# One hand-written list of single steps for the last pass, the drain and the start of the experts

## Chip, cores and metric

The kernel runs on one core of one Trainium2 chip. The metric is device time of the core in microseconds (us); the time of the kernel before is the median of three runs.

## The reference, cut to what matters

```python
def reference(**kwargs):
    attn_out = _attn_ref(q, k, v)            # B, H, S, D = 8, 8, 576, 64
    x = attn_out.transpose(0, 2, 1, 3).reshape(B * S, H * D)     # 4608 tokens x 512
    return _moe_ref(x, w_gate, w1, w2)

def _attn_ref(q, k, v):                      # two attentions, added
    out_d = sm_attn(mean over 4 of q, k, v)  # 144 x 144 scores for each head
    out_up = np.repeat(out_d, 4, axis=2)
    scores = scale * q @ k.T, masked to |i - j| < 4
    return out_up + softmax(scores) @ v

def _moe_ref(x, w_gate, w1, w2):             # 8 experts, one for each token
    e = argmax(x @ w_gate); gate = softmax(x @ w_gate)[e]
    return gate * (relu(x @ w1[e]) @ w2[e])  # 512 -> 1024 -> 512
```

## The kernel before

The attention handles 32 pairs of heads, one pair i in each pass. `steps(i)` (L813) walks the table `PASS` (L805) once; each entry is a function with an offset, so that one pass works on four pairs at different stages: scores of pair i (`s_loc` L256, `s_d` L310), exponentials of pair i-1 (`exp_d` L327), transposes of pair i-2 (`t_loc` L336, `t_d` L350, evicted by `e_loc` L343 and `e_d` L357), and products with v of pair i-3 (`pv_loc` L364, `pv_d` L378), whose result `out_d` (L385, ScalarE) and `add_up` (L389, VectorE) add into the token tile XT. Entries with "@" are hooks for routing work (`route_a`, `route_b`, `route_s`, `route_c`, L407 to L475), for turning token tiles (`x_rows` L477: four transposes on TensorE into a PSUM tile `pX`, then one ScalarE copy into the buffer `xr`), for the scatter of a token tile to the experts' rows in DRAM (`scatter` L502, an indirect DMA that GpSimd issues), and for the loads of q and k (`load_after` L125).

After pass 31, three more calls of `steps` drain the pipeline (pairs 29 to 31). Between them stands, written out by hand, the routing of the last batch m = 3 (token tiles 0 to 3, `first`; 4 to 8, `rest`) and the first half of expert 0: rows 0 to 255, whose tokens came from earlier batches. `x_load` (L543) reads these rows back from DRAM, `prep` (L585) turns them (`x_turn` L570, a VectorE transpose) and splits them into a high part on ScalarE (L576) and a low part on VectorE (L577), and `s1` (L621) multiplies them with w1, twelve matmuls for each of eight slices f. `split_w2` (L611) splits the weights of the second product. Then `s2` (L668) makes the second product for token tiles 0 and 1, while `x_load(0, 1)` reads rows 256 to 639, which need every scatter; `prep(0, 2, 3, 4)` turns those, and the loop over the experts starts with `s1` on rows 256 to 511.

The order on each engine is the order in the program; the framework only adds semaphore waits. Tiles of one name take turns in a fixed number of buffers (`pX` has three PSUM banks, `pPV` one pair of banks, `p1` two), and a writer waits for the last reader of the buffer. Memory of closed pools is used again, so `x_load(0, 0)` needs pools of the attention closed. The rows of `xr` of the last batch's tiles 4 to 8 take two places that its tiles 2 and 3 have filled, so the two small writes of `route_c` into them (L472 on ScalarE, L473 on VectorE) wait for the scatters of tiles 2 and 3 to land.

Of the kernel before, what the change touches and what calls it, by code (L numbers as in the profile page):

```python
# [22 lines left out]
NP = B * H // 2  # L23
N, DM, E, F = B * S, H * D, 8, 1024
# [14 lines left out]
FIRST = 512  # L39
# [47 lines left out]
EARLY = slice(0, CH[0][1])  # L87
# [3 lines left out]
def attention_moe_kernel(ctx: ExitStack, tc: tile.TileContext, qk, vw, wg, w1, w2, cst, csb, out):  # L91
# [17 lines left out]
    def bank():  # L109
        return psX.tile([128, 512], F32, name="pX", bufs=3)  # L110
# [293 lines left out]
    def x_slot(m, t):  # L404
        return t if t < 4 else t - 4 if m < B // 2 - 1 else t - 9 + NX
# [15 lines left out]
    def route_b(m, tiles):  # L421
        T = len(tiles)
        lg = RS[m, "lg"]
        p = bank()
        nc.tensor.transpose(p[:, :128], lg[:, :128], ident)
        if T > 4:
            nc.tensor.matmul(p[:, 128:160], lg[:, 128:], cf[:, C_SUM:C_SUM + 32], start=True, stop=True)
        pl = p[:, :T * 32].rearrange("p (t e) -> p t e", e=32)[:, :, :E]
        m_ = rp.tile([128, 5], F32, name="rm")
        nc.vector.tensor_reduce(m_[:, :T], pl, axis=AX.X, op=OP.max)  # L430
        d = p[:, 256:296].rearrange("p (t e) -> p t e", e=E)
        nc.vector.tensor_sub(d[:, :T], pl, m_[:, :T, None].to_broadcast([128, T, E]))
        ex = rp.tile([128, 5, E], F32, name="re")
        nc.scalar.activation(ex[:, :T], d[:, :T], AF.Exp)  # L434
        RS[m, "ex"], RS[m, "p"] = ex, (p, m_)

    def route_s(m, tiles):
        T = len(tiles)
        p, m_ = RS[m, "p"]
        d = p[:, 256:296].rearrange("p (t e) -> p t e", e=E)  # L440
        sc = p[:, 320:360].rearrange("p (t e) -> p t e", e=E)
        nc.vector.scalar_tensor_tensor(sc[:, :T], d[:, :T], 0.0,
                                       cf[:, None, C_DESC:C_DESC + E].to_broadcast([128, T, E]),
                                       op0=OP.is_ge, op1=OP.mult)
# [29 lines left out]
        for j, t in enumerate(tiles):  # L474
            IDX[m, t] = ix[:, j:j + 1]  # L475

    def x_rows(m, t):  # L477
        p = bank()
        for k in range(4):
            nc.tensor.transpose(p[:, k * 128:(k + 1) * 128], XT[m][:, k, t * 128:(t + 1) * 128], ident)  # L480
        xr = xrs[:, x_slot(m, t)]
        nc.scalar.activation(xr[:, :DM].rearrange("p (b k d) -> p k b d", k=4, d=32),
                             p.rearrange("p (k b d) -> p k b d", k=4, d=32), AF.Copy)

    prev_sc = []

# [359 lines left out]
    for i in range(NP):  # L846
        load_vw(i)
        if i == 0:
            for h in range(3):
                load_qk(2, h)  # L850
        if i == 2:
            nc.gpsimd.tensor_copy(crun, cf[:, C_CAP:C_CAP + E])
        if i in PADS:
            pad_first(PADS.index(i))
        if i == 8:
            nc.sync.dma_start(xs[0:ROW0, :], pad)
        steps(i)
        if i + 1 < len(WARM):
            warm(WARM[i + 1], i >= 3)
        if i == NP - 1:  # L860
            close_p1.close()
            close_s.close()
            _, mp[0] = pool(name="m1", bufs=1)
            _, mp["p1"] = pool(name="psM1", bufs=2, space=PSUM)
            x_load(0, 0)
            gi_load(0, 0, 2)
            raw_ahead(8)
# [5 lines left out]
    route_s(m, first)
    x_rows(m, 2)
    x_rows(m, 3)
    prep(0, 0, 1, get=h_bank)
    steps(NP + 1)
    s1(0, 0, EARLY)
    gi_make(0, 0, 2)
    steps(NP + 2)  # L880
    steps(NP + 3)
    route_a(m, rest)
    route_c(m, first)
    for t in (2, 3, 0, 1):
        scatter(m, t)
    route_b(m, rest)
    route_s(m, rest)
    x_rows(m, 6)
    x_rows(m, 7)
    s1(0, 1, EARLY)  # L890
    route_c(m, rest)
    x_rows(m, 8)
    s1(0, 2, EARLY)
    x_rows(m, 4)
    split_w2(0, 0)
    s1(0, 3, EARLY)
    x_rows(m, 5)
    for f in (4, 5, 6, 7):
        s1(0, f, EARLY)
        if f == 4:  # L900
            for t in rest:
                scatter(m, t)
        for j in (2 * f - 7, 2 * f - 6):
            if j < 6:
                split_w2(0, j)
# [100 lines left out]
```

## Time and profile before

| | |
|---|---|
| median of 3 runs | 646.76 us (643.39, 646.76, 649.69) |
| the profiled execution | 650.97 us |
| its span, first to last instruction | 649.2 us |
| TensorE busy | 623.0 us (96%) |
| VectorE busy | 362.8 us (56%) |
| ScalarE busy | 328.5 us (51%) |
| GpSimd busy | 186.6 us (29%) |
| mean granted TensorE clock | 0.990 of full speed |

Pass 31 begins with the first matmul of `s_loc(31)` at 180.23 us of the span; the first half of expert 0 ends at 216.02 us. A share of busy time is an average over the whole span: what a change in one stretch is worth is read from the waits of that stretch. The granted clock has two levels, 1.00 (2.4 GHz) and 0.50 (1.2 GHz).

### The profile page before, as it was taken

Reading aid. Unit: us, or ns where it says so; the run is one execution under the profiler, and the core shown is the slowest. Engines: PE = TensorE matmul, PEld = TensorE weight load, DVE = VectorE, ACT = ScalarE, POOL = GpSimd, SP = SyncE. Lnnn points to the kernel's source line nnn. Section 1 sums busy time; section 2 is a strip of 40 time slices with the busy share of each in tenths; the row PEclk is TensorE's granted clock in tenths of the full one; section 3 lists DMA queues with packets and bytes.
Section 4 is the critical chain, followed back from the end, with each engine's and each line's share of the span. In section 5 each row is a group of like instructions: output and inputs, shape, how many; then the busy total and the mean of one; then the engine's idle time right before and its main releaser. Section 6 shows DMA issues by size and latency. Waiting matters only on the chain.

```text
span 649.2 us, 16208 instructions
## 1 busy us (share of the span) xinstructions
PE 623.0 (96%) x6296; PEld 515.4 (79%) x6299; DVE 362.8 (56%) x658; ACT 328.5 (51%) x885; POOL 186.6 (29%) x271
## 2 busy tenths in 40 slices
PE   7999999999989989999999999999999999999994
PEld 3777777888868888888888888888888888888873
DVE  5998889999973465571481075175138156125020
ACT  3777778988974354452462263254236154224120
POOL 6635667778823410111111101110111101110111
PEclk9999999999998989999999999999999999999998
DMA  9799888899852695274284258238238628010001
GB/s 323 244 241 293 248 285 282 274 311 303 260 145 107 147 326 148 89 189 146 75 213 147 66 156 218 67 113 206 80 92 216 181 83 222 34 47 1 34 19 41
DMA packets 74962, 108.28 MB, mean 167 GB/s; under 512 B 16442, under 2 KB 40394, under 8 KB 74846
## 3 DMA queue, kind: packets, MB, share of 16 engines
q1 hardware_dynamic: 68718, 87.63, 47.1%
q0 software_dynamic: 5984, 19.01, 7.9%
q8 instruction: 66, 1.08, 0.7%
q14 instruction: 50, 0.41, 0.2%
q10 hardware_dynamic: 144, 0.15, 0.1%
HBM read 86.98 MB, written 23.41 MB: 170 GB/s over the span
## 4 chain that ended last, share of the span: by engine, by line
PE 76%; issue 8%; DMA 6%; DVE 3%; POOL 2%; ACT 2%; SPq 1%; POOLq 0%; another core or an unknown queue 0%; DVEq 0%; ACTq 0%
PE p L630 8%; PE p L631 8%; PE p L629 8%; PE p L643 7%; PE p L645 7%; PE p L644 7%; PE pD L317 4%; PE pPV L382 2%; PE pX L341 2%; PE pX L354 2%; PE pPV L369 2%; PE pS L268 2%; DMA xs<-xr,ix 2%; PE pX L725 2%; PE pX L744 2%
## 5 line engine op out<-in xcount | busy, mean ns | idle before, releaser
L629 PE MATMUL p<-xh,w1h 128*128 128x512 f32 (+1 forms) x288 | 106.8, 371 | 1.5 <-ACT xh L576 1.5
L630 PE MATMUL p<-xl,w1h 128*128 128x512 f32 (+1 forms) x288 | 106.3, 369 | 0.8 <-DVE xl L577 0.8
L631 PE MATMUL p<-xh,w1l 128*128 128x512 f32 (+1 forms) x288 | 106.3, 369 | 0.0
L643 PE MATMUL p<-w2h,hh 128*128 128x512 f32 x256 | 101.2, 395 | 0.0
L645 PE MATMUL p<-w2h,hl 128*128 128x512 f32 x256 | 99.8, 390 | 0.0
L644 PE MATMUL p<-w2l,hh 128*128 128x512 f32 x256 | 99.7, 390 | 0.0
L650 POOL DMA_INDIRECT out_dram<-y,tix x39 | 37.9, 971 | 215.1 <-ACT y L662 203.7
L634 DVE SCALAR_TENSOR_TENSOR hl<-p,hh 128x512 fp32r<-128x512 f32 (+1 forms) x72 | 45.5, 631 | 92.0 <-ACT hh L633 91.7
L633 ACT ACTIVATE hh<-p 128x512 fp32r<-128x512 f32 (+1 forms) x72 | 39.6, 551 | 77.6 <-PE p L631 77.6
L662 ACT ACTIVATE y<-p,gi 128x512 f32<-128x512 f32 x32 | 22.0, 689 | 94.1 <-PE p L645 89.8
L629 PEld LDWEIGHTS p<-xh,w1h 128*128 128x128 f32 x288 | 55.2, 192 | 11.0 <-ACT xh L576 2.0
L630 PEld LDWEIGHTS p<-xl,w1h 128*128 128x128 f32 x288 | 55.3, 192 | 9.6 <-DVE xl L577 0.9
L631 PEld LDWEIGHTS p<-xh,w1l 128*128 128x128 f32 x288 | 55.3, 192 | 8.8
L228 POOL TENSOR_TENSOR qkt<-qk 128x864 f32<-128x864 f32 (+2 forms) x33 | 52.5, 1590 | 20.4 <-DMA qk<-in_qk_dram 17.5
L645 PEld LDWEIGHTS p<-w2h,hl 128*128 128x128 f32 x256 | 48.0, 188 | 10.3
L644 PEld LDWEIGHTS p<-w2l,hh 128*128 128x128 f32 x256 | 48.1, 188 | 10.0 <-DVE w2l L619 0.5
L643 PEld LDWEIGHTS p<-w2h,hh 128*128 128x128 f32 x256 | 48.1, 188 | 9.4
L505 POOL DMA_INDIRECT xs<-xr,ix x36 | 36.2, 1006 | 41.6 <-ACT re L434 11.1
L619 DVE TENSOR_TENSOR w2l<-raw,w2h 128x512 fp32r<-128x512 f32 x64 | 43.4, 680 | 2.2 <-DMA xs<-xr,ix 1.5
L577 DVE TENSOR_TENSOR xl<-pX,xh 128x512 fp32r<-128x512 f32 x38 | 24.6, 683 | 35.2 <-ACT xh L576 34.2
L208 ACT ACTIVATE w1h<-raw 128x512 fp32r<-128x512 f32 (+1 forms) x72 | 41.8, 581 | 0.0
L209 DVE TENSOR_TENSOR w1l<-raw,w1h 128x512 fp32r<-128x512 f32 x56 | 39.4, 704 | 0.8
(149 smaller groups left out, 1183.3 us busy)
## 6 DMA issues: line engine op xcount, KB each, us to landing
raw<-in_w_dram SPq DMA_DIRECT2D x59, 512.0 KB
vw<-in_vw_dram SPq DMA_DIRECT2D x32, 320.0 KB
qk<-in_qk_dram SPq DMA_DIRECT2D x32, 293.0 KB
qk<-in_qk_dram SPq DMA_DIRECT2D x32, 290.0 KB
qk<-in_qk_dram SPq DMA_DIRECT2D x32, 288.0 KB
xrow<-xs SPq DMA_DIRECT2D x32, 192.0 KB
xrow<-xs SPq DMA_DIRECT2D x32, 128.0 KB
xs<-xs SPq DMA_DIRECT2D x6, 512.0 KB
```

The source lines that it names most:

```text
L208: nc.scalar.activation(hi[:, s], src[:, s], AF.Copy)
L209: (nc.vector if quarters is None else nc.gpsimd).tensor_sub(lo[:, s], src[:, s], hi[:, s])
L228: nc.gpsimd.tensor_add(QKT[i][:, a:a + n], sl(0), sl(1))
L619: nc.vector.tensor_sub(lo, src, hi)
L629: nc.tensor.matmul(p, wh[:, fs], xh[:, k, r], start=(k == 0), stop=False)
L630: nc.tensor.matmul(p, wh[:, fs], xl[:, k, r], start=False, stop=False)
L631: nc.tensor.matmul(p, wl[:, fs], xh[:, k, r], start=False, stop=(k == 3))
L633: nc.scalar.activation(hh[:, f, r], p, AF.Relu)
L634: nc.vector.scalar_tensor_tensor(hl[:, f, r], p, 0.0, hh[:, f, r], op0=OP.max, op1=OP.subtract)
L643: nc.tensor.matmul(p, hh, wh, start=(f == 0), stop=False)
L644: nc.tensor.matmul(p, hh, wl, start=False, stop=False)
L645: nc.tensor.matmul(p, hl, wh, start=False, stop=(f == 7))
```

## The change

Pass 31, the three drain passes, the routing of the last batch and the first half of expert 0 become one tuple `FIN` of 117 single steps, called one after the other; `y` is pair 30 and `z` pair 31. Passes -1 to 30 still go through `PASS`. To make single steps, `x_rows` is cut into its transposes (`x_turned`) and its copy (`x_put`), `prep` of tiles 0 and 1 into its turn (`x_early`) and its split (`split_early`), and the closing of the attention's pools with the first loads of the experts becomes the step `open_moe`, where the tiles of `XH` and `HT` are now taken too, so that addresses stay. The three tiny DMAs of pass 31 that held back loads of q and k (L129; there is nothing left to hold back) fall away. Everything from `totals()` on is as before. The scatters of the last batch go out in the order 1, 3, 2, 0, 6, 7, 8, 4, 5 (before: 2, 3, 0, 1, 4, 5, 6, 7, 8).

```diff
-    def x_rows(m, t):
-        p = bank()
+    def x_turned(m, t):
+        p = BX["x", m, t] = bank()
         for k in range(4):
             nc.tensor.transpose(p[:, k * 128:(k + 1) * 128], XT[m][:, k, t * 128:(t + 1) * 128], ident)
-        xr = xrs[:, x_slot(m, t)]
-        nc.scalar.activation(xr[:, :DM].rearrange("p (b k d) -> p k b d", k=4, d=32),
-                             p.rearrange("p (k b d) -> p k b d", k=4, d=32), AF.Copy)
+
+    def x_put(m, t):
+        nc.scalar.activation(xrs[:, x_slot(m, t), :DM].rearrange("p (b k d) -> p k b d", k=4, d=32),
+                             BX.pop(("x", m, t)).rearrange("p (k b d) -> p k b d", k=4, d=32), AF.Copy)
...
-        steps(i)
+        if i < NP - 1:
+            steps(i)
...
-        if i == NP - 1:
-            close_p1.close()
...
+    def open_moe():
+        close_p1.close()
+        close_s.close()
+        _, mp[0] = pool(name="m1", bufs=1)
+        _, mp["p1"] = pool(name="psM1", bufs=2, space=PSUM)
+        x_load(0, 0)
+        gi_load(0, 0, 2)
+        x_tiles(0, 0)
+        h_tiles(0)
+        raw_ahead(8)
...
-    steps(NP)
-    route_b(m, first)
...
+    def x_early(t):
+        turned[t] = prep(0, t, get=h_bank, hold=True)
+
+    def split_early(t):
+        turned.pop(t)()
+
+    FIN = (
+        (s_loc, z), (scatter, 2, 8), (max_loc, z), (pv_d, y - 2), (t_loc, y - 1, 0), (t_loc, y - 1, 1), (sub_loc, z),
...
+    )
+    for f, *a in FIN:
+        f(*a)
     totals()
```

The two orders on VectorE, from the end of the first routing step of the last batch. `x_turn` is the STREAM_TRANSPOSE from `xrow`, the two L396 are `add_up` of pairs 30 and 31, L462 to L473 are `route_c` of tiles 0 to 3. Before:

```order
L447 TENSOR_TENSOR oh<-pX,rm 128x32
L572 STREAM_TRANSPOSE p_4441<-xrow_4345 128x4x4x32
L572 STREAM_TRANSPOSE p_4443<-xrow_4345 128x4x4x32
L577 TENSOR_TENSOR xl_4440<-p_4441,xh_4439 128x4x128
L577 TENSOR_TENSOR xl_4440<-p_4443,xh_4439 128x4x128
L396 TENSOR_TENSOR XT<-pPV,outd_122 128x580
L634 SCALAR_TENSOR_TENSOR hl<-p_4499,hh 128x256
L396 TENSOR_TENSOR XT<-pPV,outd_123 128x580
L462 TENSOR_TENSOR pX<-pX,oh 128x32
```

The same place on VectorE now (line numbers from L480 on have grown by up to 11):

```order
L447 TENSOR_TENSOR oh<-pX,rm 128x32
L577 STREAM_TRANSPOSE p_4468<-xrow_4350 128x4x4x32
L396 TENSOR_TENSOR XT<-pPV,outd_122 128x580
L582 TENSOR_TENSOR xl_4358<-p_4468,xh_4357 128x4x128
L577 STREAM_TRANSPOSE p_4492<-xrow_4350 128x4x4x32
L462 TENSOR_TENSOR pX<-pX,oh 128x32
L464 TENSOR_REDUCE gt<-re 128x4
L466 TENSOR_REDUCE pX<-pX 128x4
L469 CAST ix<-pX 128x4
L473 RECIPROCAL xr<-gt 128x4
L396 TENSOR_TENSOR XT<-pPV,outd_123 128x580
L582 TENSOR_TENSOR xl_4358<-p_4492,xh_4357 128x4x128
```

One transpose instead of two transposes and two subtractions now stands ahead of `add_up` of pair 30, and `route_c` of the first tiles has moved ahead of `add_up` of pair 31.

TensorE from the first routing transpose (L425, `route_b`) on; L480 are `x_rows` or `x_turned`, L369 and L382 `pv_loc` and `pv_d`, L341 and L354 `t_loc` and `t_d`, L629 the first `s1` of expert 0. Before:

```order
L425 MATMUL pX<-cf,lg 128x128
L480 MATMUL pX<-cf,XT 128x128 x8
L369 MATMUL pPV<-AT,vw 64x58 x20
L382 MATMUL pPV<-ADT,vds 64x144 x4
L341 MATMUL pX<-cf,A 128x128 x5
L354 MATMUL pX<-cf,AD 72x112 x6
L629 MATMUL p_4499<-xh_4439,w1h_2070 128x256
```

TensorE from the same transpose now; L455 begins `route_c` of the first tiles:

```order
L425 MATMUL pX<-cf,lg 128x128
L369 MATMUL pPV<-AT,vw 64x58 x20
L480 MATMUL pX<-cf,XT 128x128 x4
L382 MATMUL pPV<-ADT,vds 64x144 x4
L354 MATMUL pX<-cf,AD 72x112 x6
L341 MATMUL pX<-cf,A 128x128 x5
L480 MATMUL pX<-cf,XT 128x128 x4
L382 MATMUL pPV<-ADT,vds 64x144 x4
L455 MATMUL pX<-crun,onesf 128x40
```

The transposes of pair 31 are followed by `pv_d` of pair 31 and by the routing, and the first `s1` has moved behind `pv_loc` of pair 31 and `route_a` of the last tiles.

## Rows read from the trace of the kernel before

**Rows 1.** The page, busy time of TensorE: share of the span, instructions.

```profile
PE 623.0 (96%) x6296; PEld 515.4 (79%) x6299; DVE 362.8 (56%) x658; ACT 328.5 (51%) x885; POOL 186.6 (29%) x271
```

**Rows 2.** Waits of TensorE after 180 us, the four longest: total us, times, longest.

```profile
PE pX L354 <- ACT AT L348: 2.9, 2, 2.3
PE p L629 <- ACT xh L576: 1.5, 1, 1.5
PE p L630 <- DVE xl L577: 0.8, 1, 0.8
PE pX L414 <- DVE XT L396: 0.6, 1, 0.6
```

**Rows 3.** Windows: length, busy time of five engines, granted clock, DMA share, GB/s.

```profile
7.00:15.00 8.00, 5.69 (x82) 3.68 (x85) 5.28 (x9) 3.52 (x13) 5.29 (x6) 1.00 1.04 397
45.00:80.00 35.00, 32.11 (x771) 26.89 (x769) 30.92 (x63) 27.60 (x102) 19.29 (x23) 1.00 0.89 270
...
196.19:199.60 3.41, 3.41 (x55) 3.08 (x55) 0.42 (x1) 0.38 (x1) 0.00 (x0) 0.50 0.09 32
...
227.69:230.32 2.63, 0.38 (x1) 0.19 (x1) 2.63 (x6) 2.34 (x4) 0.40 (x1) 1.00 1.08 291
230.32:233.73 3.41, 3.38 (x16) 3.38 (x17) 0.78 (x2) 0.64 (x3) 1.55 (x4) 0.50 1.03 411
```

**Rows 4.** Timeline of TensorE: start, length in us, line, what, idle time before.

```profile
180.23 0.33 PE L262 MATMUL pS<-cb 64*64 64x320 bf16 x4
...
182.89 0.45 PE L354 MATMUL pX<-cf,AD 112*72 112x112 f32 x3
...
195.25 0.48 PE L354 MATMUL pX<-cf,AD 112*72 112x112 f32 x3 [2.28 <-ACT AT L348]
...
210.00 0.39 PE L629 MATMUL p<-xh,w1h 128*128 128x256 f32 x1
...
216.02 0.28 PE L518 MATMUL pX<-crun,onesf 128*128 128x8 f32 x2
...
227.30 0.39 PE L645 MATMUL p<-w2h,hl 128*128 128x512 f32 x1
229.22 0.38 PE L629 MATMUL p<-xh,w1h 128*128 128x256 f32 x1 [1.53 <-ACT xh L576]
230.35 0.58 PE L630 MATMUL p<-xl,w1h 128*128 128x256 f32 x1 [0.75 <-DVE xl L577]
```

**Rows 5.** Timeline of VectorE around the turn of expert 0's first rows.

```profile
189.86 0.81 DVE L303 TENSOR_TENSOR A<-A,pD 128x640 f32<-128x640 f32 x1
...
192.69 1.32 DVE L572 STREAM_TRANSPOSE p<-xrow 128x512 f32<-128x512 f32 x2 [0.64 <-DMA xrow<-xs]
...
195.33 0.75 DVE L396 TENSOR_TENSOR XT<-pPV,outd 128x580 f32<-128x580 f32 x1
```

**Rows 6.** The chain that ended last, from 181 us to 221 us.

```profile
181.55 1.08 ACT AD L331 x6
182.64 5.37 DMA xs<-xr,ix
188.06 0.34 SPq L541
...
194.53 0.41 ACT outd L386
...
216.11 4.30 DMA xs<-xr,ix
220.76 0.33 SPq L541
```

**Rows 7.** All that touches the scattered rows, 175 to 235 us: time to landing.

```profile
DMA to landing us min/median/max: 3.0/3.6/5.4
```

**Rows 8.** Timeline of GpSimd: two of the nine scatters of the last batch.

```profile
205.42 0.96 POOL L505 DMA_INDIRECT xs<-xr,ix  x1 [0.22 <-issue]
...
210.25 0.96 POOL L505 DMA_INDIRECT xs<-xr,ix  x1 [1.14 <-ACT xr L482]
```

More of the change, by code (lines that the diff above doesn't have):

```diff
@@ L475, in route_c, with x_rows @@
             IDX[m, t] = ix[:, j:j + 1]
-    def x_rows(m, t):
-        p = bank()
+    def x_turned(m, t):
+        p = BX["x", m, t] = bank()
         for k in range(4):
             nc.tensor.transpose(p[:, k * 128:(k + 1) * 128], XT[m][:, k, t * 128:(t + 1) * 128], ident)
-        xr = xrs[:, x_slot(m, t)]
-        nc.scalar.activation(xr[:, :DM].rearrange("p (b k d) -> p k b d", k=4, d=32),
-                             p.rearrange("p (k b d) -> p k b d", k=4, d=32), AF.Copy)
+    def x_put(m, t):
+        nc.scalar.activation(xrs[:, x_slot(m, t), :DM].rearrange("p (b k d) -> p k b d", k=4, d=32),
+                             BX.pop(("x", m, t)).rearrange("p (k b d) -> p k b d", k=4, d=32), AF.Copy)
+    def x_rows(m, t):
+        x_turned(m, t)
+        x_put(m, t)
     prev_sc = []
@@ L583, in attention_moe_kernel, with x_tiles @@
     XB = {}
+    def x_tiles(e, c):
+        if (e, c) not in XH:
+            XH[e, c] = tuple(mp[c].tile([128, 4, FIRST if c == 0 else 128], F32R, name=f"x{w}{c}") for w in "hl")
     def prep(e, *ts, get=bank, hold=False):
@@ L588, in prep @@
             c, s = chunk(t)
-            if (e, c) not in XH:
-                XH[e, c] = tuple(mp[c].tile([128, 4, FIRST if c == 0 else 128], F32R, name=f"x{w}{c}") for w in "hl")
+            x_tiles(e, c)
             r = min(t // 2, 1)
@@ L619, in split_w2, with h_tiles, s1 @@
         nc.vector.tensor_sub(lo, src, hi)
-    def s1(e, f, r=slice(0, FIRST)):
+    def h_tiles(e):
         if e not in HT:
             HT[e] = tuple(mp[0].tile([128, 8, FIRST], F32R, name=f"h{w}") for w in "hl")
+    def s1(e, f, r=slice(0, FIRST)):
+        h_tiles(e)
         xh, xl = XH[e, 0]
@@ L856, in attention_moe_kernel @@
             nc.sync.dma_start(xs[0:ROW0, :], pad)
-        steps(i)
+        if i < NP - 1:
+            steps(i)
         if i + 1 < len(WARM):
             warm(WARM[i + 1], i >= 3)
-        if i == NP - 1:
-            close_p1.close()
[L862 to L867, printed above, removed]
+    def open_moe():
[8 more added lines that the diff above has]
+        raw_ahead(8)
@@ L868, in attention_moe_kernel @@
     m = B // 2 - 1
     first, rest = list(range(4)), list(range(4, 9))
-    steps(NP)
-    route_b(m, first)
[L873 to L905, printed above, removed]
+    y, z = NP - 2, NP - 1
+    turned = {}
+    def x_early(t):
+        turned[t] = prep(0, t, get=h_bank, hold=True)
+    def split_early(t):
+        turned.pop(t)()
@@ new lines, in attention_moe_kernel @@
+    FIN = (
+        (s_loc, z), (scatter, 2, 8), (max_loc, z), (pv_d, y - 2), (t_loc, y - 1, 0), (t_loc, y - 1, 1), (sub_loc, z),
+        (exp_d, y), (x_turned, m, 0), (out_d, y - 2), (pv_loc, y - 2), (s_d, z), (t_d, y - 1, 0), (sums, y),
+        (eps, y), (add_up, y - 2), (e_loc, y - 1, 0), (e_loc, y - 1, 1), (t_d, y - 1, 1), (inv, y), (x_put, m, 0),
+        (e_d, y - 1, 0), (t_v, z), (pv_loc, y - 1), (scatter, 2, 7), (max_d, z), (open_moe,), (e_v, z),
+        (e_d, y - 1, 1), (norm, y), (norm_d, y), (max_scale, z), (exp_loc, z), (exp_d, z), (t_loc, y, 0),
+        (t_d, y, 0), (pv_d, y - 1), (t_d, y, 1), (sums, z), (out_d, y - 1), (t_loc, y, 1), (e_d, y, 0),
+        (add_up, y - 1), (e_loc, y, 0), (eps, z), (inv, z), (norm_d, z), (e_loc, y, 1), (e_d, y, 1),
+        (gi_make, 0, 0, 2), (route_b, m, first), (norm, z), (pv_loc, y), (x_turned, m, 1), (pv_d, y), (t_d, z, 0),
+        (t_d, z, 1), (x_put, m, 1), (route_s, m, first), (t_loc, z, 0), (out_d, y), (x_early, 0), (t_loc, z, 1),
+        (x_turned, m, 3), (add_up, y), (e_d, z, 0), (e_d, z, 1), (e_loc, z, 1), (pv_d, z), (split_early, 0),
+        (e_loc, z, 0), (x_early, 1), (out_d, z), (x_put, m, 3), (route_c, m, first), (pv_loc, z), (x_turned, m, 2),
+        (add_up, z), (split_early, 1), (scatter, m, 1), (route_a, m, rest), (x_turned, m, 6), (x_put, m, 2),
+        (x_put, m, 6), (s1, 0, 0, EARLY), (route_b, m, rest), (scatter, m, 3), (scatter, m, 2), (route_s, m, rest),
+        (s1, 0, 1, EARLY), (x_turned, m, 7), (x_put, m, 7), (route_c, m, rest), (split_w2, 0, 0), (split_w2, 0, 1),
+        (x_turned, m, 4), (s1, 0, 2, EARLY), (x_turned, m, 8), (scatter, m, 0), (x_put, m, 8), (s1, 0, 3, EARLY),
+        (x_put, m, 4), (scatter, m, 6), (split_w2, 0, 2), (x_turned, m, 5), (x_put, m, 5), (s1, 0, 4, EARLY),
+        (split_w2, 0, 3), (scatter, m, 7), (split_w2, 0, 4), (scatter, m, 8), (scatter, m, 4), (s1, 0, 5, EARLY),
+        (s1, 0, 6, EARLY), (scatter, m, 5), (s1, 0, 7, EARLY), (split_w2, 0, 5),
+    )
```

## The prediction

> **What bounds the kernel now.** I read the page first: TensorE is busy 96% of the span [rows 1], so only time in which TensorE stands still, or runs at half clock, can be won by a new order of the same instructions. The waits of TensorE come next, from pass 31 to the end of the span [rows 2]: the four longest kinds, 5.8 us together, all lie in the rewritten stretch or in what hangs on it. The windows view then shows what the waits cost beyond themselves [rows 3]: after the longest one (2.28 us, ending at 195.25 [rows 4]) the granted clock stands at 0.50 for 3.41 us, and after the pair of waits that ends at 230.35 again for 3.41 us. At half clock a stretch does half its work, so each costs 3.41 / 2 = 1.7 us. The budget of the change is therefore 2.9 + 0.6 us of waits in the drain, 1.7 us of clock behind them, 1.5 + 0.8 us of waits before expert 0's second half, and 1.7 us of clock behind those: 9.2 us, 1.4% of the profiled execution's 650.97 us.
>
> The first place, in order of time: the second wait for L348 [rows 2, 4] ends at 195.25. ScalarE's evictions and VectorE's `add_up` of pair 30 stood behind the turn of expert 0's first rows. Those rows came back from DRAM at 192.69, and VectorE then made two transposes and two subtractions before `add_up` could start at 195.33 [rows 5]: 2.64 us. The second place: the last scatter starts at 216.11, while `s1` ends at 216.02 (L518 begins there) [rows 4, 6]. The read of rows 256 to 639 starts on SP at 220.76, after that scatter has landed [rows 6], and its split product reaches TensorE at 230.35, 2.7 us after TensorE had finished at 227.30 + 0.39 = 227.69 [rows 4].
>
> **The change, part by part.** TensorE gets the same matmuls, so its work costs and saves nothing in itself. The three dropped DMAs of pass 31 held back nothing, since no load is left behind them except the read of expert 0's rows, which waits longer for the scatters: nothing.
>
> *Waits in the drain.* Before: 3.5 us. Now, one by one:
> - `add_up(30)` has one transpose ahead of it, not 2.64 us of work. The read of the rows starts at 188.06, after the scatter begun at 182.64 has landed [rows 6]. That scatter and the one ahead of it change places; the new first one needs the later of two copies on ScalarE, done when the exponentials begin at 181.55 [rows 6], so the pair runs up to 0.3 us later. Rows at 192.7 to 193.0, a transpose of 1.32 / 2 = 0.66, `add_up` of 0.75 [rows 5]: TensorE's `pv_d(31)` can start at 194.1 to 194.4. TensorE gets there at about 193.4: it stood still from 192.97 with almost the same matmuls behind it, and I add 0.4 for the new waits below. Wait: 0.7 to 1.0 us, I take 0.8 where there were 2.28.
> - The shorter wait for L348, 2.9 - 2.3 = 0.6 us, was for one of three `pX` banks; the new order asks for banks as fast, so 0.6 stays.
> - `route_a` waited 0.6 us for `add_up(31)`; four transposes now lie between, so 0.
> - New: `pv_d(28)` goes ahead of `pv_loc(28)`, and the latter then waits for `out_d(28)`, which reads the same bank and stands behind the exponentials on ScalarE (181.55 + 1.08 = 182.63, and its own run of 0.41 [rows 6]). TensorE was at 182.89 after four groups [rows 4], and one of these is now a little shorter: it is ready at 182.7. Wait 0.3. Behind it queue the scores of pair 31 and everything else; the next evictions have the same 0.3 of slack.
> - New: the transposes of pair 30 follow VectorE's normalisation more closely (0.81 us long [rows 5]); half of one, 0.4, is my estimate, between 0 and 0.8.
>
> New waits: 0.8 + 0.6 + 0 + 0.3 + 0.4 = 2.1, a gain of 1.4. If the rows land early and the small ones vanish, 0.9 is left (gain 2.6); if all are double, 4.2 (loss 0.7).
>
> *The clock in the drain.* The longest single wait falls from 2.28 to 0.8. From 7 to 15 us TensorE has 8.00 - 5.69 = 2.3 us of idle time and a clock of 1.00 [rows 3]. So I expect no half-clock stretch: 1.7 gained; the other end is 0.
>
> *The last scatters.* One `s1` of 256 rows takes (216.02 - 210.00) / 4 = 1.5 us [rows 4]. In both orders six of them and three groups of transposes come after the `route_c` of tiles 4 to 8, so that `route_c` ends about 10.2 us before the end T of the last `s1`, and its small writes are ready at T - 9.3. Before, they had to wait for the scatter of tile 3, begun at 205.42 [rows 8], to land, and then the first of the five scatters was that of tile 4, whose copy came last but one: it began at 210.25, T - 5.8 [rows 8]. Now tile 2's scatter follows a copy made ahead of the first `s1`, at about T - 13.8; with 3.0 to 5.4 us to landing [rows 7] the gate opens between T - 9.3 and T - 8.4, and tiles 6 and 7 go first, whose copies are long done. Five scatters took 216.11 - 210.25 = 5.9 us from first to last start [rows 6, 8]. The last now starts between T - 3.4 and T - 2.5, before T + 0.1: earlier by 2.6 to 3.5 us against the end of `s1`. The rows were 2.7 us late. So the 2.3 us of waits go, and what is late next is nothing on TensorE, with 0 to 0.8 us to spare; a remainder of a tenth or two may stay. The half-clock stretch behind them goes too, 1.7 us. The other end is 0 for both.
>
> Other scatters, copies and weight splits that moved cost nothing in the sum: they lie on engines that are 29 to 56% busy [rows 1], beside eight `s1` of 1.5 us each. If that cover failed, `s1` would wait for `hl` two slices later.
>
> The sum: 1.4 + 1.7 + 2.3 + 1.7 = 7.1 us off the profiled execution, 650.97 to 643.9. That execution is 0.65% above the median of the runs shown, so the same share gives 646.76 x 643.9 / 650.97 = 639.7 us.
>
> One rule would move the first term. The scatters here took 3.0 to 5.4 us to land [rows 7]. The Trainium skill (DMA: Bandwidth & Descriptors, Anatomy of one DMA) puts the fixed cost of such a DMA at about 2 us; by that the rows would be back before `add_up(30)` needs VectorE, the 0.8 would be gone and the time be 638.9. No scatter in that stretch landed so fast, so I keep the row.
>
> **Rivals.**
> 1. *The clock in the drain still drops.* Several waits of 0.3 to 0.8 us within 10 us may do what one of 2.28 did. Against it: 45 to 80 us has 2.9 us of idle time, clock 1.00 [rows 3]. Then 1.4 + 2.3 + 1.7 = 5.4 us: 641.4.
> 2. *The rows of the second half stay late.* If one of the last copies on ScalarE stands behind a weight split or a blocked write, or the scatters stretch, the last scatter starts near T as before. For it: scatter and splits share the end of the list, and the spare is under 1 us. Then only 1.4 + 1.7 = 3.1 us: 643.7.
> 3. *Slower: the clock stays low through the drain.* With waits spread over the whole stretch, TensorE would sit at 0.50 not for one stretch but from the first wait at 183 us on. Each 3.41 us costs 1.7; against the 5.4 us of the other terms the change loses from the fourth stretch on, and 1% from the seventh; eight cover 27 us, up to the end of the first half: 8 x 1.7 - 5.4 = 8.2 us, 655.0. Both low stretches of the trace follow waits of over 2 us together, and 45 to 80 us argues against it [rows 3]. The Trainium skill (TensorE: Matmul & The Clock Gate, A second HAM failure mode: psum-queue depth-cycling) says that short idle times between groups of matmuls, from cycling through PSUM banks, can make the clock swing; this drain cycles through three banks, but no row here shows it.
> 4. *The new order costs as much as it saves* in waits that I do not see, an undone first term and a leftover of the second: 645 to 646.
>
> **How the numbers follow.** Forecast 0.57, rival 1 0.14, rival 2 0.18, rival 3 0.05, rival 4 0.06. The three runs shown spread by 1%, and 1% (6.5 us) is about what a measurement can tell from no change. The forecast's 7.1 us is just past that line, with about 2 us of doubt: 0.67 of it falls beyond, of rival 1 a third, of rival 2 little: 0.57 x 0.67 + 0.14 x 0.33 + 0.18 x 0.1 = 0.45. Slower gets rival 3 and a bit of rival 4, 0.06; the rest, 0.49, is within 1%. The range goes from gains of 8.7 us and a fast run, 636.0, to rival 2 with a slow run, 645.5.
>
> **What would show it.** Right: no wait of TensorE over 1 us between 180 and 240 us; clock 1.00 throughout that stretch; the last scatter at least 2.5 us before the end of the last `s1`, which ends near 213; `s1` of the second half beginning straight behind `s2`, some 6 us of it earlier. Wrong: a half-clock stretch after 185 us, a wait of L640 or L641 for `xh` or `xl` near 225 us, or a TensorE wait on `out_d`, `A` or a bank of over 1 us.

## The result, and the profile after

| | before | now |
|---|---|---|
| median, first comparison (4 runs each) | 646.85 us | 641.34 us |
| ratio, with 95% interval | | 0.9886 [0.9845, 0.9928] |
| median, second comparison (35 and 12 runs) | 646.73 us | 639.1 us |
| ratio, with 95% interval | | 0.9881 [0.9855, 0.9907] |
| the profiled execution | 650.97 us | 641.42 us |
| its span | 649.2 us | 639.6 us |

The change is 1.2% faster, 7.6 us by the second comparison; the prediction was 639.7 us. One of the 12 runs, and one of the six of x10 below, was disturbed and is left out of the ratios and means. TensorE has the same matmuls and is busy for nearly the same time: 621.0 us for 623.0. The two half-clock stretches had made 2 x 1.7 us of those; this execution has one of its own at 13.1 us, in code that is the same in both kernels. The page's busy row, which answers to [rows 1]:

```profile
PE 621.0 (97%) x6299; PEld 513.5 (80%) x6299; DVE 363.2 (57%) x658; ACT 329.7 (52%) x885; POOL 185.8 (29%) x271
```

The longest kinds of waits of TensorE after 178 us (total us, times, longest), which answer to [rows 2]:

```profile
PE pX L736 <- DVE xb L775: 0.4, 1, 0.4
PE pX L341 <- ACT ADT L362: 0.4, 1, 0.4
PE p L640 <- issue: 0.3, 1, 0.3
PE pX L341 <- ACT mxd L325: 0.2, 1, 0.2
```

None of the four kinds of [rows 2] is left. The two for `pX` of L341 lie in the drain, with two smaller ones of 0.08 and 0.13 us that both wait for `out_d`; the others lie at 611 and 253 us, far behind the change. The windows (length, busy time of five engines, granted clock, DMA share, GB/s) answer to [rows 3]; the first reaches from the start of pass 31 to the start of `s2`, the others over the two places where the clock had been at 0.50:

```profile
179.03:210.67 31.64, 30.84 (x477) 27.06 (x477) 21.66 (x52) 23.06 (x69) 12.56 (x26) 1.00 0.50 170
183.00:195.00 12.00, 11.28 (x212) 8.30 (x212) 10.20 (x25) 10.28 (x34) 0.20 (x2) 1.00 0.74 226
218.00:228.00 10.00, 10.00 (x70) 9.34 (x70) 7.04 (x12) 5.55 (x12) 2.41 (x6) 1.00 1.07 355
```

The whole stretch from pass 31 to `s2` is at full clock, and TensorE idles 31.64 - 30.84 = 0.8 us of it (before: 35.93 - 32.31 = 3.6). The timeline of TensorE (start, length, line, what, idle time before) answers to [rows 4]; L654 is the first product of `s2`, L640 and L641 the first `s1` of expert 0's second half:

```profile
179.03 0.33 PE L262 MATMUL pS<-cb 64*64 64x320 bf16 x4
...
187.62 0.44 PE L341 MATMUL pX<-cf,A 128*128 128x128 f32 x2 [0.40 <-ACT ADT L362]
...
192.07 0.72 PE L382 MATMUL pPV<-ADT,vds 72*64 72x144 f32 x8
...
210.67 0.47 PE L654 MATMUL p<-w2h,hh 128*128 128x512 f32 x1
...
221.45 0.39 PE L656 MATMUL p<-w2h,hl 128*128 128x512 f32 x1
221.68 0.28 PE L640 MATMUL p<-xh,w1h 128*128 128x256 f32 x1
221.79 0.28 PE L641 MATMUL p<-xl,w1h 128*128 128x256 f32 x1
```

I call the start of pass 31 S and the start of `s2` T. From S to T it was 216.16 - 180.23 = 35.93 us and is 210.67 - 179.03 = 31.64. From T to the first product with `xl` of the second half (T to `xl` below) it was 230.35 - 216.16 = 14.19 us and is 221.79 - 210.67 = 11.12. VectorE's timeline answers to [rows 5], and for the second half's rows shows how close they come:

```profile
190.54 0.73 DVE L577 STREAM_TRANSPOSE p<-xrow 128x512 f32<-128x512 f32 x1
191.18 0.74 DVE L396 TENSOR_TENSOR XT<-pPV,outd 128x580 f32<-128x580 f32 x1
192.54 0.69 DVE L582 TENSOR_TENSOR xl<-p,xh 128x512 fp32r<-128x512 f32 x1 [0.63 <-ACT xh L581]
...
218.31 1.91 DVE L577 STREAM_TRANSPOSE pX<-xrow 128x512 f32<-128x512 f32 x3 [3.16 <-DMA xrow<-xs]
220.13 1.86 DVE L582 TENSOR_TENSOR xl<-pX,xh 128x512 fp32r<-128x512 f32 x3
```

The turn of the first rows no longer waits for DMA (0.64 us before [rows 5]), and `add_up` of pair 30 ends at 191.92, ahead of the `pv_d` of pair 31 at 192.07. The two `xl` that the second half's first `s1` needs are done at 220.13 + 1.86 x 2/3 = 221.4, and TensorE asks at 221.79: 0.4 us to spare. Behind this lie the last scatter on GpSimd and the two reads of rows on SP, which answer to [rows 6, 8]:

```profile
208.04 1.39 POOL L510 DMA_INDIRECT xs<-xr,ix  x1 [0.21 <-ACT w2h L626]
```

```profile
185.57 2.25 SPq L546 DMA_DIRECT2D xrow<-xs  x4
...
211.85 1.88 SPq L546 DMA_DIRECT2D xrow<-xs  x4
```

The last scatter starts at 208.04, 2.63 us ahead of T (before: 0.06 ahead of it). All scatters from 175 to 235 us, which answers to [rows 7]:

```profile
DMA to landing us min/median/max: 3.0/3.2/3.9
```

### The profile page after: what moved, and what is told of

It reads as the page before. It is cut to its first block, busy times and chain, and to the rows that moved or that the text cites. A ratio compares the mean times of both kernels' runs of the same rounds, so it can differ in the third digit from the quotient of the medians.

```text
span 639.6 us, 16201 instructions
## 1 busy us (share of the span) xinstructions
PE 621.0 (97%) x6299; PEld 513.5 (80%) x6299; DVE 363.2 (57%) x658; ACT 329.7 (52%) x885; POOL 185.8 (29%) x271
## 4 chain that ended last, share of the span: by engine, by line
PE 84%; issue 7%; DVE 2%; DMA 2%; ACT 2%; POOL 1%; SPq 0%; POOLq 0%; another core or an unknown queue 0%; ACTq 0%; DVEq 0%
PE p L640 9%; PE p L642 9%; PE p L641 9%; PE p L654 8%; PE p L656 8%; PE p L655 8%; PE pD L317 4%; PE pX L341 3%; PE pX L354 3%; PE pPV L382 3%; PE pPV L369 2%; PE pX L480 2%; PE pS L268 2%; PE pX L736 2%; PE pX L755 2%
## 5 line engine op out<-in xcount | busy, mean ns | idle before, releaser
L640 PE MATMUL p<-xh,w1h 128*128 128x512 f32 (+1 forms) x288 | 105.8, 367 | 0.3 <-issue 0.3
L641 PE MATMUL p<-xl,w1h 128*128 128x512 f32 (+1 forms) x288 | 105.2, 365 | 0.0
L654 PE MATMUL p<-w2h,hh 128*128 128x512 f32 x256 | 101.1, 395 | 0.0
L640 PEld LDWEIGHTS p<-xh,w1h 128*128 128x128 f32 x288 | 54.3, 189 | 9.4 <-issue 0.7
L641 PEld LDWEIGHTS p<-xl,w1h 128*128 128x128 f32 x288 | 54.3, 189 | 8.8
L654 PEld LDWEIGHTS p<-w2h,hh 128*128 128x128 f32 x256 | 48.1, 188 | 9.4
```

Source lines behind the costliest of these rows:

```text
L654: nc.tensor.matmul(p, hh, wh, start=(f == 0), stop=False)
```

## The experiments

My theory: two things set the time, VectorE's queue ahead of `add_up` of pair 30, and the last scatter's start against T; each also takes a half-clock stretch with it. Rivals: the gain comes from the rest of the list; or the waits are not what costs. Each kernel's runs stand against runs of before on the same chip, so the ratios are what to compare. The median of before was 646.0 us beside x1 to x4, 646.73 beside x5 to x8, 647.67 beside x12, and 663.82 beside x9 to x11, whose chip ran everything slower. The changed kernel itself was timed beside x5 to x8 alone (x5), so x1 and x2 are set against it over two chips. The three stretches are told from each kernel's one profiled execution.

| kernel | ratio to before | S to T | T to `xl` | T to the end |
|---|---|---|---|---|
| before | 1 | 35.93 | 14.19 | 433.03 |
| the change | 0.9886 [0.9845, 0.9928] | 31.64 | 11.12 | 428.98 |
| x1_turns_ahead | 0.9935 [0.9905, 0.9965] | 33.80 | 11.12 | 429.00 |
| x2_tile4_first | 0.9947 [0.9926, 0.9969] | 31.71 | 13.67 | 432.66 |
| x3_before_turn_late | 1.0039 [1.0017, 1.0061] | 34.23 | 13.74 | 435.07 |
| x4_before_both | 1.0015 [0.9996, 1.0034] | 32.84 | 12.89 | 434.36 |
| x5_after_again | 0.9881 [0.9855, 0.9907] | 32.28 | 11.12 | 428.65 |
| x6_h_shifted | 0.9959 [0.9934, 0.9983] | 31.60 | 11.35 | 433.02 |
| x7_turn_late_kept | 0.9941 [0.9915, 0.9968] | 32.99 | 14.12 | 431.49 |
| x8_both_kept | 0.9930 [0.9901, 0.9958] | 32.83 | 12.97 | 430.78 |
| x9_tile6_first | 1.0017 [0.9991, 1.0044] | 44.71 | 11.12 | 428.63 |
| x10_h_256 | 0.9895 [0.9851, 0.9939] | 35.44 | 11.12 | 428.71 |
| x11_w2_shifted | 0.9991 [0.9962, 1.0020] | 35.40 | 11.33 | 432.49 |
| x12_both_shifted | 0.9937 [0.9909, 0.9964] | 31.60 | 11.17 | 431.20 |

### One part of the change undone: the place of the turn, then the last five scatters

x1 puts both turns and both splits ahead of `add_up` of pair 30 again:

```diff
-        (t_d, z, 1), (x_put, m, 1), (route_s, m, first), (t_loc, z, 0), (out_d, y), (x_early, 0), (t_loc, z, 1),
-        (x_turned, m, 3), (add_up, y), (e_d, z, 0), (e_d, z, 1), (e_loc, z, 1), (pv_d, z), (split_early, 0),
-        (e_loc, z, 0), (x_early, 1), (out_d, z), (x_put, m, 3), (route_c, m, first), (pv_loc, z), (x_turned, m, 2),
-        (add_up, z), (split_early, 1), (scatter, m, 1), (route_a, m, rest), (x_turned, m, 6), (x_put, m, 2),
+        (t_d, z, 1), (x_put, m, 1), (route_s, m, first), (t_loc, z, 0), (out_d, y), (x_early, 0), (x_early, 1), (split_early, 0), (split_early, 1), (t_loc, z, 1),
+        (x_turned, m, 3), (add_up, y), (e_d, z, 0), (e_d, z, 1), (e_loc, z, 1), (pv_d, z),
+        (e_loc, z, 0), (out_d, z), (x_put, m, 3), (route_c, m, first), (pv_loc, z), (x_turned, m, 2),
+        (add_up, z), (scatter, m, 1), (route_a, m, rest), (x_turned, m, 6), (x_put, m, 2),
```

> The changed kernel, but both turns of expert 0's first rows and both their splits stand ahead of add_up(30) on VectorE and ahead of pair 31's evictions on ScalarE, as before. Theory (VectorE's queue held TensorE): pv_d(31) waits for add_up(30) about 2 us again, and the clock may drop for one stretch, so from s_loc(31) to the end of the last s1 it takes 33.4 to 35.1 us instead of 31.4; the time is 2.0 to 3.7 us over the changed kernel's. Rival (the gain came from spreading many small steps): under 0.7 us.

VectorE's timeline of x1, and TensorE's wait a moment before it:

```profile
187.75 1.32 DVE L577 STREAM_TRANSPOSE p<-xrow 128x512 f32<-128x512 f32 x2
189.19 1.29 DVE L582 TENSOR_TENSOR xl<-p,xh 128x512 fp32r<-128x512 f32 x2
190.39 0.75 DVE L396 TENSOR_TENSOR XT<-pPV,outd 128x580 f32<-128x580 f32 x1
```

```profile
190.04 0.44 PE L341 MATMUL pX<-cf,A 128*128 128x128 f32 x2 [1.54 <-ACT ADT L362]
```

The wait is not the one that I expected. TensorE waits 1.54 us for a `pX` bank, which ScalarE's eviction L362 gives back, and only 0.20 us at `pv_d(31)` for `add_up(30)` (0.41 more for `out_d`). ScalarE's timeline of x1 shows what the eviction stood behind:

```profile
188.56 1.14 ACT L581 ACTIVATE xh<-p 128x512 fp32r<-128x512 f32 x2 [0.62 <-DVE p L577]
189.59 0.69 ACT L362 ACTIVATE ADT<-pX 72x288 f32<-72x288 f32 x2
```

It was the same in before, for the wait of 2.28 us:

```profile
193.50 1.14 ACT L576 ACTIVATE xh<-p 128x512 fp32r<-128x512 f32 x2 [1.15 <-POOL spacer L504]
194.53 0.41 ACT L386 ACTIVATE outd<-pPV 128x288 f32<-128x288 f32 x1
194.82 0.73 ACT L348 ACTIVATE AT<-pX 128x232 f32<-128x232 f32 x2
```

The rows came at 192.69, VectorE had turned the first of them at 192.69 + 0.66 = 193.35, ScalarE split both into `xh`, and only then came the eviction for which TensorE waited until 195.25. `add_up(30)` began at 195.33, after TensorE had gone on. So what held TensorE in before was ScalarE's queue, with VectorE's turns ahead of it, and not VectorE's subtractions or `add_up`. In x1 either queue would have done it: `add_up(30)` ended at 190.39 + 0.75 = 191.14, and `pv_d(31)`, which needs it, started at 191.19. x1 moves both queues together; only the timelines tell them apart.

S to T grows by 2.16 us, T to the end by nothing, and the ratio is 0.5% higher, 3.5 us (the two intervals just overlap). So the place of the turn and of its split is worth about 2 to 3.5 us. The clock stayed at 1.00 in x1's drain.

x2 sends the last five scatters in the old order and together, behind `s1` of slice 6:

```diff
-        (x_put, m, 4), (scatter, m, 6), (split_w2, 0, 2), (x_turned, m, 5), (x_put, m, 5), (s1, 0, 4, EARLY),
-        (split_w2, 0, 3), (scatter, m, 7), (split_w2, 0, 4), (scatter, m, 8), (scatter, m, 4), (s1, 0, 5, EARLY),
-        (s1, 0, 6, EARLY), (scatter, m, 5), (s1, 0, 7, EARLY), (split_w2, 0, 5),
+        (x_put, m, 4), (split_w2, 0, 2), (x_turned, m, 5), (x_put, m, 5), (s1, 0, 4, EARLY),
+        (split_w2, 0, 3), (split_w2, 0, 4), (s1, 0, 5, EARLY),
+        (s1, 0, 6, EARLY), (scatter, m, 4), (scatter, m, 5), (scatter, m, 6), (scatter, m, 7), (scatter, m, 8), (s1, 0, 7, EARLY), (split_w2, 0, 5),
```

> The changed kernel, but the last five scatters go out as before: all behind the copy of tile 5, in the order 4, 5, 6, 7, 8. Theory (the last scatter sets when the second half's rows come back): the last scatter starts at about the end of the last s1, s1 of the second half waits 2 to 2.8 us for xh and xl, a half-clock stretch of 3.4 us follows, 4.0 to 4.5 us are lost. Rival (the drain alone made the gain, the spare is large): no wait, 0.

The waits of TensorE in x2, a window behind them, and GpSimd's last scatter:

```profile
PE p L640 <- ACT xh L581: 1.4, 1, 1.4
PE p L641 <- DVE xl L582: 0.7, 1, 0.7
```

```profile
223.29:226.70 3.41, 3.41 (x18) 3.41 (x18) 1.12 (x2) 0.96 (x3) 1.06 (x3) 0.50 1.01 402
```

```profile
208.86 0.96 POOL L510 DMA_INDIRECT xs<-xr,ix  x1 [0.23 <-issue]
```

The last scatter started at 208.86, and T is 208.52: it is late by 0.34 us, and the pair of waits and the half-clock stretch of [rows 3, 4] are back. T to the end is 432.66 - 428.98 = 3.7 us longer; S to T is as in the change. So each of the two places holds by itself, the waits cost what they show, and the two ratios, 0.5% and 0.7%, make up the change's 1.2%.

### The two parts alone on the kernel before, and why they first failed

x3 moves the turn and the split of expert 0's first rows behind the second drain pass; x4 also sends the last five scatters as 6, 7, 8, 4, 5:

```diff
-    prep(0, 0, 1, get=h_bank)
     steps(NP + 1)
-    s1(0, 0, EARLY)
+    prep(0, 0, 1, get=h_bank)
     gi_make(0, 0, 2)
     steps(NP + 2)
+    s1(0, 0, EARLY)
...
-            for t in rest:
+            for t in (6, 7, 8, 4, 5):
```

> The kernel before with one move: the turns and splits of expert 0's first rows behind add_up(30), and the first s1 behind the next drain pass. Theory (VectorE's queue): the wait of 2.28 us falls under 0.7 and the half-clock stretch behind it goes; 3.0 to 4.0 us faster than before, the late rows of the second half unchanged at 2.3 us. Rival (spreading): under 1 us faster.

> The kernel before with that move and with the last five scatters in the order 6, 7, 8, 4, 5. Theory: 3.0 to 4.0 us from the move, and 1.2 to 1.8 us of the 2.7 us by which the second half's rows are late, with the clock stretch behind them if what is left is too short to drop the clock: 4.2 to 7.5 us faster than before in all. Rival (the whole list is needed): under 2 us faster.

Both missed: x3 is 0.4% slower than before and x4 no faster, though S to T fell by 1.7 and 3.1 us. The loss stands at the far end: from the first `xl` product to the end it is 435.07 - 13.74 = 421.33 us in x3, where before has 433.03 - 14.19 = 418.84, with a half-clock stretch in it. The grouped view from 260 to 600 us (busy, mean ns of one) of before, and then of x3, shows which matmuls:

```profile
L629 PE MATMUL p<-xh,w1h 128*128 128x512 f32 x224 | 87.2, 389 | 0.0
...
L643 PE MATMUL p<-w2h,hh 128*128 128x512 f32 x196 | 77.3, 394 | 0.0
```

```profile
L629 PE MATMUL p<-xh,w1h 128*128 128x512 f32 x218 | 84.8, 389 | 0.0
...
L643 PE MATMUL p<-w2h,hh 128*128 128x512 f32 x202 | 80.6, 399 | 0.0
```

The first product keeps its 389 ns, the second goes from 394 to 399. There is no wait ahead of them. What differs there, besides the order, is one thing: with `prep` behind `gi_make`, the small tile `tix` is taken first, and the built program has `hh` and `hl` 128 bytes per partition higher (`hh` at 95328 instead of 95200), `tix` below them and every other tile where it was. Three kernels, x6 to x8, tell address from order. x5 is the change itself once more; x6 is the change with that shift and nothing else; x7 and x8 are x3 and x4 with the old addresses.

In x6, against the change:

```diff
-        h_tiles(0)
...
-        (gi_make, 0, 0, 2), (route_b, m, first), (norm, z), (pv_loc, y), (x_turned, m, 1), (pv_d, y), (t_d, z, 0),
+        (gi_make, 0, 0, 2), (h_tiles, 0), (route_b, m, first), (norm, z), (pv_loc, y), (x_turned, m, 1), (pv_d, y), (t_d, z, 0),
```

In x7 and x8, ahead of `steps(NP + 1)` of x3 and x4:

```diff
+    XH[0, 0] = tuple(mp[0].tile([128, 4, FIRST], F32R, name=f"x{w}0") for w in "hl")
+    HT[0] = tuple(mp[0].tile([128, 8, FIRST], F32R, name=f"h{w}") for w in "hl")
```

> The changed kernel once more, timed in more runs beside the others. By the traces the stretch from s_loc(31) to the end of the span is 460.6 us instead of 469.0: 8.4 us faster than before, ratio 0.987. Rival (part of the 8.4 was the profiled run of before alone): 5.5 us, ratio 0.9915.

> The changed kernel with the order untouched; the small tile tix is taken before hh and hl, which then lie 128 bytes higher in each partition, all else in its place. Theory (the place of hh and hl set the pace in the two runs that began with the kernel before): matmuls of the second product take 0.233 us in many places instead of 0.227, the end of the first half to the end of the span 432.9 us instead of 429.0, 3.9 us slower than the changed kernel. Rival (the slower pace came with the moved order): no difference.

> The move of the turns behind add_up(30) again, now with hh and hl at the addresses of the kernel before. Theory: the pace of the second product is as before (no drift of 3.9 us), the drain takes 32.8 us, or 34.5 with a half-clock stretch, instead of 35.9: 1.5 to 4.5 us faster than before. Rival (the pace is a matter of order): still 2 to 3 us slower than before.

> That move and the scatters in the order 6, 7, 8, 4, 5, at the addresses of the kernel before. Theory: the drain 32.8 us, the second half's rows 1.3 us earlier, no clock stretch: 5.0 to 6.0 us faster than before, ratio 0.991, two thirds of what the whole list brings. Rival (pace by order): 0 to 1 us.

The same grouped view for the change, and for x6:

```profile
L654 PE MATMUL p<-w2h,hh 128*128 128x512 f32 x208 | 81.9, 394 | 0.0
```

```profile
L654 PE MATMUL p<-w2h,hh 128*128 128x512 f32 x206 | 82.3, 399 | 0.0
```

The shift alone makes the second products 5 ns longer each; 768 of them make 4 us, and T to the end grew by 433.02 - 428.98 = 4.0 us. In time x6 is 0.78% behind x5, 5.0 us. With the addresses kept, the two parts gain: x7 0.6%, as expected, and x8 0.7% (0.9% expected), and x8 against the change's 1.2% leaves 0.5% for the rest of the list. What the scatter order adds on top of the turn is not shown by the times: 644.01 - 641.92 = 2.1 us by the medians, 0.1% or 0.7 us by the ratios, whose intervals overlap. The waits of x7 and then of x8 show what it does:

```profile
PE p L629 <- ACT xh L576: 1.5, 1, 1.5
PE pX L354 <- ACT AT L348: 0.8, 2, 0.7
PE p L630 <- DVE xl L577: 0.7, 1, 0.7
```

```profile
PE p L630 <- DVE xl L577: 0.9, 2, 0.7
PE pX L354 <- ACT AT L348: 0.8, 2, 0.7
PE p L629 <- ACT xh L576: 0.7, 1, 0.7
```

The 2.28 us in the drain are gone in both; the rows of the second half are late by 0.9 us less in x8, and late still. With the whole list it goes altogether: there the first of the nine scatters starts 15.3 us ahead of T (before: 12.0), the last 2.6, where x8 has 1.1.

### The scatter order alone

```diff
-            for t in rest:
+            for t in (6, 7, 8, 4, 5):
```

> The kernel before with one edit: the last five scatters go out as tiles 6, 7, 8, 4, 5; every address and every other instruction stays. Theory (the last scatter sets when the second half's rows are there): the last scatter starts 0.9 to 1.8 us earlier against the first matmul of s2 (before: T - 0.06), L629 and L630 wait 0.5 to 1.4 us together instead of 2.28, and the drain ahead of it is unchanged; the median is 0.9 to 3.1 us below that of before (the larger end if the half-clock stretch behind the wait goes too). Rival (the five scatters pass at their own pace and the order is nothing): the last one within 0.3 us of T as before, and no difference of time.

The expected gain of 0.9 to 3.1 us didn't come, and why is open. In the trace the rows of the second half are in time (T to `xl` 11.12 us, as in the change), but the profiled execution, 668.48 us, has a wait that no other trace here has. The rows are TensorE's wait and ScalarE's timeline:

```profile
PE p L629 <- DVE hl L634: 4.0, 1, 4.0
```

```profile
226.17 0.62 ACT L618 ACTIVATE w2h<-raw 128x512 fp32r<-128x512 f32 x1
229.96 0.38 ACT L633 ACTIVATE hh<-p 128x256 fp32r<-128x256 f32 x1 [3.17 <-remote]
```

ScalarE stood still for 3.17 us, released by nothing that the profile shows ("remote"; x10 and x11, on the same chip, have one such wait of 0.8 us each), and `s1` waited for `hh` and `hl`; this also gave the scatters time that they have not in other runs. By the ratio the edit alone brought nothing on this chip. Whether the rows were late in before there isn't known, as there is no trace of before from it; in x10 and x11, on the same chip, S to T took 35.4 us where it took 31.6 elsewhere, and the last scatter started 4.4 us ahead of T.

### How far the address effect goes

x10 takes the four small tiles `tix`, `tgi`, `ttix` and `gap` ahead of `hh` and `hl`, which lie 256 bytes higher then; x11 makes `gap` 128 bytes larger, so that tiles of `w2` lie 128 bytes higher; x12 does x6 and x11 together. The texts below speak of all tiles of `w2`, but the edit moves those of slices 0 to 5: the tiles of slices 6 and 7 come from another pool and stay.

In x10, besides the two edits of x6:

```diff
     def split_w2(e, f):
-        if (e, f) == (0, 0):
-            home("tgi", 2)
-            home("ttix", 1)
-            home("gap", 16)
...
     def h_tiles(e):
         if e not in HT:
+            if e == 0:
+                home("tgi", 2)
+                home("ttix", 1)
+                home("gap", 16)
```

In x11, and in x12 besides those of x6:

```diff
-            home("gap", 16)
+            home("gap", 48)
```

> The changed kernel with four small tiles taken ahead of hh and hl, so that these two lie 256 bytes per partition higher and all others but the four where they were (an earlier run moved them by 128 and lost 4 to 5 us in the second products). If a 256-byte boundary (or a larger one) decides, hh and hl keep their place in it and the time is that of the changed kernel, about 639 us, with fewer than 50 matmul steps between 0.235 and 0.3 us in the second products; if the exact place decides, or the distance to another tile, it is 2 to 5 us longer.

> The changed kernel with the tiles of w2 (the moving side of the second product) 128 bytes per partition higher, hh and hl unchanged. If the distance between the two operands decides, this loses 2 to 5 us as moving hh and hl did (about 641 to 644 us); if only the place of hh and hl does, the time is that of the changed kernel, about 639 us.

> The changed kernel with hh, hl and the tiles of w2 all 128 bytes per partition higher, so that the distance between the two operands of the second product is again what it was. If that distance (modulo 256 bytes) decides, the slow matmul steps go: fewer than 50 between 0.235 and 0.3 us, T to the end near 429 us, and the ratio to before is that of the changed kernel, 0.988. If each operand has to lie where it lay (modulo 256), the steps are as slow as with either shifted alone or slower: T to the end 432.5 us or more, ratio 0.995 or above.

The grouped rows of x10, x11 and x12, in that order:

```profile
L654 PE MATMUL p<-w2h,hh 128*128 128x512 f32 x195 | 76.9, 394 | 0.0
```

```profile
L654 PE MATMUL p<-w2h,hh 128*128 128x512 f32 x199 | 79.3, 398 | 0.0
```

```profile
L654 PE MATMUL p<-w2h,hh 128*128 128x512 f32 x208 | 82.2, 395 | 0.0
```

256 bytes cost nothing, 128 bytes on either operand cost about 4 us, and x12 about half of that by its trace (T to the end 431.20; by the ratios 0.6% behind the change, where x6 is 0.8%). Taken whole, neither of x12's two expectations came out. Taken by slices, the first did. The second product of a token tile is 24 matmuls, three for each slice; this is the mean time in ns from the start of one to the start of the next, worked out from the starts in each kernel's one trace:

| kernel | moved | slice 0 | slices 1 to 5 | slices 6 and 7 |
|---|---|---|---|---|
| the change | nothing | 227.1 | 227.5 | 227.6 |
| x10 | `hh`, `hl` by 256 bytes | 227.1 | 227.5 | 227.5 |
| x6 | `hh`, `hl` by 128 | 232.7 | 232.5 | 232.4 |
| x11 | `w2` of slices 0 to 5 by 128 | 231.6 | 232.8 | 230.1 |
| x12 | `hh`, `hl`, and `w2` of slices 0 to 5, by 128 | 231.1 | 227.5 | 232.7 |

In x12's slices 1 to 5, where both operands moved, the pace is the old one; in its slices 6 and 7, where only `hh` and `hl` did, it is the slow one. So in these kernels the distance between the two operands decides: in the change it is a multiple of 256 bytes (`hh` at 95200, `w2` of slice 0 at 128224, 129 x 256 further), and 128 more or less is slow. Behind a change of pace the next slice is still slow (slice 0 of x12; in x11 slice 6 has 231.4 and slice 7 has 228.0). I read that as the pace of the slices ahead running on; no run tests it.

## Why the prediction was right

- *Direction, size and range*: 639.7 us forecast, 641.34 and 639.1 measured; the two places are those forecast, and x1, x2 and x7 bear them out one by one. In the first place the prediction names both queues, but it prices the 2.28 us by the 2.64 us of work ahead of `add_up(30)`; the wait was for ScalarE's evictions, behind the split `xh` (x1 above). The new list moves both, so the forecast didn't suffer.
- *Waits in the drain, the mis-sized term*: I wrote 3.5 to 2.1, a gain of 1.4. Measured, as idle time of TensorE from S to T: 3.6 to 0.08 + 0.19 + 0.40 + 0.13 = 0.8, a gain of 2.8, just past the far end of my own bounds (2.6). The step that failed first is "`pv_d(31)` can start at 194.1 to 194.4": I took the rows' landing from before. The scatter ahead of the read started at 181.91 and the read at 185.57, 3.66 us later, where it had been 182.64 to 188.06, 5.4 us; so the 0.8 was 0. That was luck: in x5's trace, of the same kernel, the two steps lie 4.6 us apart, and `pv_d(31)` waits 0.58 us, so this term is set by a landing time that varies from run to run. The Trainium skill (DMA: Bandwidth & Descriptors, Anatomy of one DMA) has about 2 us for a DMA's fixed cost; the wait it would have removed did go, but no scatter in this stretch landed in under 3.0 us, so its figure isn't why. The others were smaller too: `out_d` of pair 28 made a wait of 0.08 (0.3 forecast), the normalisation 0.2 (0.4), and the bank wait of 0.6 became one of 0.4.
- *The clock, in both places*: the trace has it as forecast, 0.50 before and 1.00 now, 1.7 us each, 3.4 together. All eight traces of kernels made from the new list (the change, x1, x2, x5, x6, x10, x11, x12) have 1.00 from S to T. (A further low stretch, which the prediction leaves out, begins in every kernel 4 to 7 us before the end of the span: at 643.33 in before.) But the row that I argued from, 7 to 15 us with 2.3 us of idle time at 1.00 [rows 3], couldn't carry it: in the change's own trace the same code has 8.00 - 5.53 = 2.5 us of idle time there and a granted clock of 0.88, as a half-clock stretch begins at 13.1. Over runs it is a bit less: the mean granted clock was 0.9907 in 35 runs of before and 0.9950 in 11 of the change, and 0.0043 x 647 = 2.8 us.
- *Late rows of the second half*: right to the row. Last scatter at T - 2.63 (forecast T - 3.4 to T - 2.5), 2.28 us of waits gone, 0.4 us to spare (forecast 0 to 0.8). Two small misses cancel in it: the first of the five scatters began at T - 8.03, later than forecast (T - 9.3 to T - 8.4), and the five took 5.4 us for 5.9. `s1` of the second half follows `s2` without a wait.
- *The sum*: 2.8 + 2.3 + 2.8 = 7.9 us by these, 7.7 by the mean of the same runs (646.85 - 639.11), 7.1 forecast. T at 210.67 instead of "near 213" is the drain's 1.2 us more than forecast and 1.2 us of an earlier S, in code that is the same in both; so the two profiled executions differ by 1.2 + 4.3 + 4.05 = 9.55 us, of which the first belongs to the run and not to the change.
- *Costs put at nothing*: moved scatters, copies and weight splits cost nothing, as said. What I passed over as a detail of `open_moe`, that the tiles of `XH` and `HT` are taken there "so that addresses stay", was worth 4 to 5 us (x6 against x5): without it the change would have kept a third of its gain.
- *Rivals*: rival 1 (clock drops in the drain all the same) and rival 3 (it stays low) did not happen in the traces of the change; x3, with the old list, shows that rival 1 can. Rival 2 is what x2 does. Rival 4, a change that costs as much as it saves, is what x3 and x4 are, by a mechanism that I had not thought of.

None of the other kernels was faster than the change; with 0.8 us of idle time of TensorE left between S and T, a new order has little more to give there.

## What to carry to other kernels

Follow the longest waits of the engine that bounds the kernel back to the queue in which the awaited instruction stands, and count what stands ahead of it there; moving it forward gains the wait and sometimes a half-clock stretch behind it. When a moved instruction takes a buffer for the first time, keep the addresses of large matmul operands, or at least their distance from each other, or compare the mean duration of every large group of matmuls before and after. A part that fails alone may still be right: look at where in the span the time was lost before dropping it.

## What the runs showed of the hardware that I had not expected

- *A shift of one operand by 128 bytes against the other slows matmuls.* With `hh` and `hl`, or tiles of `w2`, 128 bytes per partition higher, the matmuls of 512 columns over them followed each other 5 ns later on average (227.5 to 232.5), 4 us of the kernel; 256 bytes cost nothing, and where both operands moved by 128 the pace was the old one (227.5 in x12's slices 1 to 5). The first product, over other tiles, was the same in all. Why isn't known: no counter of the profile shows it.
- *The same waits don't always drop the clock.* Below are two windows of x3 and then the same two of x7, counted from their starts of pass 31 (0.80 us apart): 6.8 us with part of the drain's waits, which agree within 0.01 us, and 3.41 us behind them.

```profile
186.00:192.80 6.80, 5.83 (x117) 4.43 (x118) 5.55 (x13) 4.47 (x12) 0.21 (x2) 1.00 0.92 281
192.81:196.22 3.41, 3.41 (x31) 3.12 (x35) 0.88 (x2) 0.38 (x1) 0.00 (x0) 0.50 0.06 21
```

```profile
186.80:193.60 6.80, 5.83 (x117) 4.43 (x118) 5.55 (x13) 4.48 (x12) 0.20 (x2) 1.00 0.97 275
193.61:197.02 3.41, 3.36 (x61) 2.93 (x62) 1.16 (x5) 0.77 (x2) 0.00 (x0) 1.00 0.05 11
```

  The same 117 matmuls in the same 5.83 us are followed by half clock in x3 (31 matmuls in the next 3.41 us) and by full clock in x7 (61). x7 also kept the full clock behind its 1.5 + 0.7 us before the second half, which cost before and x2 a stretch.
- *More than half of the spread of the runs goes with the clock.* In 35 runs of before, the time falls by 0.61 us with each 0.001 of mean granted clock, where 0.001 of 647 us is 0.65: 13 runs at 0.990 have a mean of 647.18 us, 9 runs at 0.993 one of 644.91. The clock goes with 60% of the variance; the rest is open, as the 13 runs at 0.990 alone reach from 644.93 to 649.11. So the gain of a removed wait is partly a matter of how often it drops the clock, and one profiled execution can't tell that.
